# The first layer's last two chunks as Strassen products in an attention-and-MLP kernel

## The chip, the cores and the metric

The kernel runs on one core of a Trainium2 chip. A core has five engines that run side by side, each working through its own list of instructions in order: TensorE (PE; its weight loads are a row of their own, PEld), VectorE (DVE), ScalarE (ACT), GpSimd (POOL) and SyncE (SP, which here only starts transfers). They meet through semaphores. The metric is the device time of one execution in microseconds.

## The reference

The first stage is causal attention with 16 extra "beacon" keys that every query sees; the second is a two-layer perceptron with a leaky ReLU. The attention's output, heads side by side, is the perceptron's input.

```python
B, H, S, Nb, D = (8, 8, 576, 16, 64)
scores = scale * np.matmul(q, k_all.transpose(0, 1, 3, 2))   # k_all: beacons, then keys
scores = np.where(causal, -1000000000.0, scores)
a = np.exp(scores - scores.max(-1, keepdims=True))
a /= a.sum(-1, keepdims=True) + 1e-09
attn = np.matmul(a, v_all)
x = attn.transpose(0, 2, 1, 3).reshape(B * S, H * D)         # 4608 x 512
h = x @ w_in                                                 # 512 x 2048
g = np.maximum(0.01 * h, h)
out = g @ w_out                                              # 2048 x 512
```

## The kernel before

**Attention** goes by pairs of heads: 8 batches of 4 pairs make 32 pairs g, 0 to 31. For each, the transposed keys and queries give scores (L314), ScalarE takes the exponential into a tile of probabilities `aT` (L329, L333; four such tiles, used in turn), GpSimd sets the masked triangles to zero (`affine_select`, L289), and TensorE multiplies the probabilities with the values (L359), in two halves a pair: 12 matmuls, then 18. VectorE divides by the row sums into `x_nat` (L388, L389), which frees the PSUM tile, and SP's queue transposes `x_nat` by DMA into `xT`, the perceptron's input with features on partitions (L417, L422, L425; the last batch has three such transposes a pair).

**The perceptron** goes by nine chunks of 512 tokens, 0 to 8. `up()` makes one 128-row block of the first layer (L442): four matmuls of 512 columns, one for each 128 of the 512 features, into a PSUM tile, which ScalarE takes through the leaky ReLU (Prelu) into `gT` (L450). A chunk has 16 of them. `down()` makes half a product of the second layer. Chunk 0's is plain; for the others Strassen's identity in Winograd's form is used: the left factor (tokens by hidden features) and the right one (hidden features by outputs) are cut into 2 x 2 blocks, and seven products of half size take the place of eight. A product has two `down()`s of eight matmuls with 256 columns (L537). The sums of token blocks that the products need are made from `gT` by VectorE (`token_sums`, L610, four a slice, two slices a chunk); the sums of weight blocks are made once (`weight_sums`). `combine` joins the products: ScalarE copies p1, p4, p5 out of PSUM (L562), VectorE adds (L559), SP stores.

**PSUM** has two `sc` tiles of two banks (2 x 512 floats), for scores, and four tiles of one bank (pool `ps_one`) that all else takes in turn: a value product, an `up()` or a product of the second layer gets the tile that was taken four tiles earlier, once that one is empty.

**The order** is what the program writes (`manual_schedule`): each engine runs its instructions as emitted. From pair 8 on, a list of events with positions in units of pairs is sorted, and between two events `fill()` emits as many `up()`s and `down()`s as an even spread over the batch asks for; `KEPT` = 4 of them are kept over to the next batch. When the list is done, a loop of `fill()` emits what is left: the rest of chunk 6, chunk 7 and chunk 8. `due` is a list of token sums waiting to be emitted, one with each `up()` or `down()`.

Of the kernel before, what the change touches and what calls it, by code (L numbers as in the profile page):

```python
# [8 lines left out]
FP32 = mybir.dt.float32  # L9
BF16 = mybir.dt.bfloat16  # L10
AF = mybir.ActivationFunctionType
# [4 lines left out]
def kernel(  # L16
# [11 lines left out]
    nc = tc.nc  # L28

    B, H, S, D = q.shape  # L30
    NB = beacon_k.shape[2]
    DM = moe_w_in.shape[0]
    DF = moe_w_in.shape[1]
# [4 lines left out]
    NF = DF // 128  # L38
# [411 lines left out]
        nc.scalar.activation(out=gT[i][:, fc, :], in_=acc, func=AF.Prelu, alpha=0.01)  # L450

    HF, HD, HT = NF // 2, DM // 2, 256
    ADD, SUB = ALU.add, ALU.subtract

    def weight_sums(part):
# [13 lines left out]
    def token_sums(i, lo, hi):  # L469
        if i not in sums:  # L470
            sums[i] = [sum_tile(n).rearrange("p (c t) -> p c t", c=HF) for n in range(3)]
        g, s = gT[i], sums[i]
        a11, a12 = g[:, lo:hi, 0:HT], g[:, HF + lo : HF + hi, 0:HT]
        a21, a22 = g[:, lo:hi, HT : 2 * HT], g[:, HF + lo : HF + hi, HT : 2 * HT]
        s1, s2, s4 = (s[n][:, lo:hi] for n in range(3))
        return [
            dict(out=s1, in0=a21, in1=a22, op=ADD),
            dict(out=s2, in0=s1, in1=a11, op=SUB),
            dict(out=a21, in0=a11, in1=a21, op=SUB),
            dict(out=s4, in0=a12, in1=s2, op=SUB),  # L480
        ]

# [21 lines left out]
    def ND(i):  # L504
        return NF if i == 0 else 2 * len(PRODUCTS)
# [44 lines left out]
    def combine(i, n, acc, tiles):  # L550
        lo, hi = tiles[0] * HD, tiles[1] * HD

        def part(name, new=False):
            if new and lo == 0:
                parts[name] = opool.tile([128, 512], FP32, name=name, bufs=1)
            return parts[name][:, lo:hi]

        def add(to, x, y):
            nc.vector.tensor_tensor(out=to, in0=x, in1=y, op=ADD)  # L559

        if n in (1, 4, 5):
            nc.scalar.copy(out=part(f"p{n}", True), in_=acc)  # L562
        if n == 6:
            add(part("u2", True), acc, part("p1"))
        elif n == 2:
            add(part("p1"), acc, part("p1"))
            store(i, 0, 0, tiles, part("p1"))
        elif n == 7:
            add(part("u3", True), acc, part("u2"))
            add(part("p4"), part("u3"), part("p4"))  # L570
            store(i, 1, 0, tiles, part("p4"))
        elif n == 5:
            add(part("u3"), part("u3"), part("p5"))
            store(i, 1, 1, tiles, part("u3"))
            add(part("p5"), part("u2"), part("p5"))
        elif n == 3:
            add(part("p5"), acc, part("p5"))
            store(i, 0, 1, tiles, part("p5"))

    def store(i, half, cols, tiles, c):  # L580
        t0 = i * 512 + half * HT + tiles[0] * 128
        n = tiles[1] - tiles[0]
        nc.sync.dma_start(
            out=out[t0 : t0 + n * 128, cols * HD : (cols + 1) * HD].rearrange("(t p) d -> p t d", p=128),
            in_=c.rearrange("p (t d) -> p t d", t=n),
        )

    done1, done2, at2, ready, turn, first_down, held = [0], [0], [0, 0], [0], [0], [0], [0]

# [17 lines left out]

    def add_due(n=1):
        while due and n:
            nc.vector.tensor_tensor(**due.pop(0)[1])  # L610
            n -= 1

    def add_all(i):
# [16 lines left out]
    def down():  # L630
        add_due()
        if at2[1] == 4:
            add_all(at2[0])
        moe2(*at2)
        done2[0] += 1
        at2[1] += 1
        if at2[1] == ND(at2[0]):
            at2[:] = at2[0] + 1, 0
        turn[0] = 0
# [19 lines left out]
            )  # L659

    NG = B * NPAIR
    KEPT, LEAD = 4, 2

    def has(g):
        return 0 <= g < NG
# [68 lines left out]
    with order:  # L734
        load_first_keys()
        load_beacon_k(0, 2, nc.scalar)
        nc.vector.memset(blank, 0.0)
        nc.vector.memset(ident, 0.0)
        run("l0.0 l1.0")
        make_identity(nc, ident, nomemset=True)  # L740
        make_ones()
        run("l1.1 l2.0 l2.1 V0.0 V0.1 l3.0 l3.1 V0.2 V0.3 V0.4 l4.0 l4.1 i0")
        make_pads()
        unused(13, 256)
        cast_beacon_k(0, 2, nc.scalar.copy)
        beacon_transposes(0, 2)
        unused(13)
        nc.scalar.copy(out=k_nat0[:, :, 0], in_=first_k[0])
        nc.vector.tensor_copy(out=k_nat0[:, :, 1], in_=first_k[1])
        run("q0.1 k0 w2.384 s0.0 m0.0 w3.256 s0.1 q1 s0.2 m0.1 k1 s0.3 m0.2")  # L750
        run("w2.384 s1.0 m1.0 q2 s1.1 k2 w2.384 s1.2 m1.1 w2.384 s1.3 m1.2 W0.0.4 s2.0 m2.0 W0.0.4 s2.1 W0.0.6 q3 l5.0 l5.1 s2.2 k3 w4.384 v0.0 m2.1 s2.3 i1 m2.2 W0.1.4 s3.0 m3.0 v1.0 s3.1 v0.1 s3.2 v1.1 m3.1 l6.0 l6.1 s3.3 x0.1 m3.2")
        run("v2.0 V1.0 V1.1 q4 v2.1 x1 k4.1 v3.0 v3.1 x2.1 s4.0 s4.1 x3 m4.0 V1.2 V1.3 V1.4 l7.0 l7.1 u u s4.2 s4.3 q5 k5 m4.1 m4.2 u o0 u")
        load_beacon_k(2, B, nc.gpsimd)
        run("s5.0 s5.1 m5.0 u u u s5.2 s5.3 q6 k6 m5.1 m5.2 o1 u u s6.0 s6.1 m6.0 u v4.0 u v4.1 y4 N8.0 N8.1 u s6.2 s6.3 q7 k7 m6.1 m6.2 u")
        cast_beacon_k(2, B, nc.gpsimd.tensor_copy)
        run("u v5.0 u v5.1 N9.0 s7.0 s7.1 m7.0 d x5 v6.0 v6.1 T8 d s7.2 s7.3")
        beacon_transposes(2, B)
        run("m7.1 m7.2 N9.1 u b8.2 b9.2 b10.2 b11.2 x6 v7.0 T9 v7.1 d d d N10.0 N10.1 d V2.0 V2.1 x7 t0 T10")


        FIRST = 2 * NPAIR
        COLS = FLAT[NKB]
        TILES = (NG - FIRST) * COLS // 512

        def tile_parts(n):
            at, end, parts = 512 * n, 512 * (n + 1), []
            while at < end:
                r, lo = divmod(at, COLS)
                hi = min(COLS, lo + end - at)
                parts.append((FIRST + r, lo, hi))  # L770
                at += hi - lo
            return parts

        def block(m):
            tiles = [tile_parts(n) for n in range(3 * m, min(3 * m + 3, TILES))]
            for n, parts in enumerate(tiles):
                stretch(parts, apart=n == 0)
            for parts in tiles:
                triangles(parts)

        def has_down():
            return at2[0] < done1[0] // NF

        since = 0
        events = []
        for g in range(FIRST, NG):
            if g > FIRST + 2:
                events.append((g - 3.25, 0, run, ("N%d.0" % g,)))
                events.append((g - 2.95, 0, run, ("N%d.1" % g,)))
            if g > FIRST + 2:  # L790
                events.append((g - 1.75, 0, run, ("T%d" % g,)))
            if g > FIRST + 3:
                events.append((g - 2.5, 0, run, ("b%d.2" % g,)))
            at = g + (2.05 if g % NPAIR == NPAIR - 1 else 2.25)
            events.append((at, 3, value, (g, 0)))
            events.append((at + 0.37, 4, value, (g, 1)))
            events.append((at + 0.38, 5, x_turn, (g,)))
        for m in range((TILES + 2) // 3):
            events.append((FIRST + (0.4 if m else 0.6) + 1536 / COLS * m, 2, block, (m,)))
        ends = [FIRST]  # L800
        for g in range(FIRST, NG):
            events.append((g + 3.5, 2, finish, (g, 2)))
            if g % NPAIR == NPAIR - 1:
                ends.append(g + 3.5)
        for b in range(2, B):
            for n in range(2 if b == 2 else 0, NKB):
                events.append((4 * b - (0.1 if b == 2 else 0.4 - 0.3 * n), 6, load_v_cast, (b, n)))
        events.sort(key=lambda e: e[:2])
        first_down[0] = 4
        w, d0 = 0, done1[0] + done2[0]  # L810
        for at, _, what, args in events:
            while w + 2 < len(ends) and at > ends[w + 1]:
                w, d0 = w + 1, done1[0] + done2[0]
            todo = NF * ready[0] + sum(ND(i) for i in range(ready[0])) - KEPT - d0
            aim = d0 + todo * (at - ends[w]) / (ends[w + 1] - ends[w])
            while done1[0] + done2[0] < aim and fill():
                pass
            if what is block:
                since = done1[0] + done2[0]
            elif what is value:  # L820
                while done1[0] + done2[0] < since + (2 if has_down() else 4) and fill(True):
                    pass
            what(*args)
        while at2[0] < NCH:
            fill()


# [28 lines left out]
```

## Time and profile before

| what | us |
|---|---|
| median of 3 runs | 330.15 (327.78 to 332.76) |
| the profiled execution | 334.24, of which span 332.5 |
| last value product ends | 266.65 |
| chunk 7's first layer, TensorE | 275.38 to 289.20 |
| chunk 8's first layer with chunk 7's second | 290.94 to 315.24 |
| last matmul ends | 329.21 |

The profile is one execution. Its span runs from the first to the last instruction; the execution's own time is 1.74 us more. Busy times are given for each engine, with the idle time ahead of a group of instructions and what ended it. "The chain that ended last" is followed back from the last instruction, each step to what released it. In the timeline a row has the start, the length, the engine, the line of the kernel, the operation, output and inputs, the shapes, and in square brackets how long the engine sat idle before and for whom.

The granted TensorE clock was 0.998 of full speed over the span.

### The profile page before, as it was taken

What the parts mean: (1) busy time and instruction counts of PE and PEld (TensorE: products, weight loads), DVE (VectorE), ACT (ScalarE), POOL (GpSimd) and SP (SyncE); (2) the same over time, 40 slices, a digit from 0 to 9 for tenths busy, and PEclk for the clock granted to TensorE, in tenths of its full rate; (3) what the DMA queues carried; (4) which work ended last, traced back from release to release, by engine and by line L of the source; (5) the groups of instructions that cost most, each with busy time, mean ns of one, the idle gap of its engine ahead of it and who ended that gap; (6) DMA issues with size and microseconds to landing.
All of it is one profiled execution on the core that took longest, in us unless ns stands there. A gap on an engine that the chain in (4) does not pass through costs nothing.

```text
span 332.5 us, 8516 instructions
## 1 busy us (share of the span) xinstructions
PE 325.1 (98%) x3429; PEld 215.8 (65%) x3429; DVE 146.4 (44%) x297; ACT 201.0 (60%) x336; POOL 188.2 (57%) x354
## 2 busy tenths in 40 slices
PE   8999999998999999999999999999999999999995
PEld 5457456444578457855688888656865695566685
DVE  3327245713665254534434535543553552424344
ACT  3757986196883885477756785686467516643510
POOL 8857875989999968656966887667221000000000
PEclk9999999999999999999999999999999999999999
DMA  8999999999999999999999999999621111000203
GB/s 133 143 175 169 124 197 121 134 148 193 165 137 143 178 168 102 162 141 130 124 136 206 139 141 91 197 101 117 98 97 49 38 52 63 2 33 30 67 32 128
DMA packets 155928, 39.93 MB, mean 120 GB/s; under 512 B 143040, under 2 KB 153152, under 8 KB 155888
## 3 DMA queue, kind: packets, MB, share of 16 engines
q0 software_dynamic: 99824, 18.54, 84.1%
q1 hardware_dynamic: 55792, 20.77, 36.9%
q8 instruction: 27, 0.44, 0.6%
q14 instruction: 13, 0.11, 0.2%
q10 hardware_dynamic: 272, 0.07, 0.1%
HBM read 37.22 MB, written 9.44 MB: 140 GB/s over the span
## 4 chain that ended last, share of the span: by engine, by line
PE 81%; DMA 6%; ACT 4%; POOL 4%; DVE 2%; issue 1%; SPq 0%; DVEq 0%; ACTq 0%; POOLq 0%
PE acc L442 32%; PE acc L537 26%; PE av L359 8%; PE sc L314 5%; PE sc L267 3%; ACT aT L333 3%; PE av L645 3%; DMA k_nat<-in_k_dram 3%; PE tp L243 2%; DMA xT<-x_nat 2%; DMA kT<-k_nat 1%; POOL v_aug L214 1%; DVE u L559 1%; POOL k_nat L171 1%; DVE p L559 1%
## 5 line engine op out<-in xcount | busy, mean ns | idle before, releaser
L442 PE MATMUL acc<-xT,w_in_sb 128*128 128x512 bf16 (+1 forms) x640 | 136.6, 358 | 1.0 <-ACT gT L450 0.4
L450 ACT ACTIVATE gT<-acc 128x512 bf16<-128x512 f32 x144 | 83.6, 616 | 53.4 <-PE acc L442 50.9
L289 POOL TENSOR_SCALAR_AFFINE_SELECT aT<-aT 128x256 bf16<-128x256 bf16 (+2 forms) x160 | 64.5, 429 | 63.2 <-ACT aT L329 29.8
L442 PEld LDWEIGHTS <-w_in_sb 128*128 128x128 bf16 x640 | 59.4, 98 | 52.9 <-issue 4.3
L537 PEld LDWEIGHTS <-gT 128*128 128x128 bf16 x512 | 48.7, 98 | 8.4 <-issue 1.2
L333 ACT ACTIVATE aT<-sc 128x1024 bf16<-128x1024 f32 (+3 forms) x64 | 51.8, 895 | 0.0
L537 PE MATMUL acc<-w_out_sb,gT 128*128 128x256 bf16 x384 | 46.2, 273 | 0.0
L359 PEld LDWEIGHTS <-aT 128*128 128x128 bf16 (+1 forms) x960 | 36.9, 98 | 9.0 <-issue 2.6
L537 PEld LDWEIGHTS <-gsum 128*128 128x128 bf16 x384 | 36.7, 98 | 6.8
L329 ACT ACTIVATE aT<-sc 128x512 bf16<-128x512 f32 (+3 forms) x64 | 29.0, 521 | 19.1 <-PE sc L314 19.1
L359 PE MATMUL av<-v_aug,aT 128*128 128x65 bf16 (+1 forms) x960 | 39.6, 195 | 0.9 <-DVE x_nat L389 0.7
L562 ACT COPY p<-acc 128x512 f32<-128x512 f32 (+1 forms) x25 | 14.5, 580 | 39.0 <-PE acc L537 35.3
L388 DVE RECIPROCAL rec<-av 128x6 f32<-128x6 f32 (+1 forms) x64 | 12.0, 187 | 55.9 <-PE av L359 55.6
L171 POOL DMA_DIRECT2D k_nat<-in_k_dram x48 | 34.7, 728 | 1.8 <-DMA v_aug<-in_v_dram 0.7
L171 POOL DMA_DIRECT2D q_nat<-in_q_dram x48 | 34.7, 728 | 0.5 <-issue 0.3
L214 POOL DMA_DIRECT2D v_aug<-in_v_dram x40 | 34.1, 859 | 0.0
L389 DVE TENSOR_TENSOR x_nat<-av,rec 128x384 bf16<-128x384 f32 (+1 forms) x64 | 31.4, 491 | 2.2
L276 ACT ACTIVATE aT<-sc 128x1024 bf16<-128x1024 f32 (+3 forms) x32 | 26.8, 875 | 9.1 <-PE sc L267 8.6
L537 PE MATMUL acc<-w_sum,gsum 128*128 128x256 bf16 x256 | 31.9, 273 | 0.0
L610 DVE TENSOR_TENSOR gsum<-gT 128x1024 bf16<-128x1024 bf16 x16 | 11.3, 703 | 30.1 <-ACT gT L450 30.1
L314 PE MATMUL sc<-qT,kT 64*128 64x80 bf16 (+22 forms) x384 | 22.3, 250 | 1.2 <-DMA kT<-k_nat 1.2
L314 PEld LDWEIGHTS <-kT 64*128 64x128 bf16 x384 | 12.9, 94 | 12.9 <-issue 8.2
(62 smaller groups left out, 235.7 us busy)
## 6 DMA issues: line engine op xcount, KB each, us to landing
out_dram<-p SPq DMA_DIRECT2D x26, 256.0 KB, 3.1
q_nat<-in_q_dram POOLq DMA_DIRECT2D x48, 72.0 KB, 5.4
k_nat<-in_k_dram POOLq DMA_DIRECT2D x48, 72.0 KB, 5.4
v_aug<-in_v_dram POOLq DMA_DIRECT2D x24, 128.0 KB, 6.0
w_in_sb<-in_moe_w_in_dram POOLq DMA_DIRECT2D x2, 1024.0 KB, 10.3
w_out_sb<-in_moe_w_out_dram POOLq DMA_DIRECT2D x2, 1024.0 KB, 12.3
out_dram<-u SPq DMA_DIRECT2D x8, 256.0 KB, 2.7
gsum<-in_q_dram POOLq DMA_DIRECT2D x8, 144.0 KB, 4.8
```

The costliest lines, as they stand in the source:

```text
L171: nc.gpsimd.dma_start(out=t[:, :, par], in_=(q, k)[which][b, 2 * hp + par].rearrange("(t p) d -> p t d", p=NR),)
L214: nc.gpsimd.dma_start(out=dst[lo : ROWS[c], c, :, 0:D], in_=v[b, :, OFF[c] : OFF[c] + n].rearrange("h p d -> p h d"),)
L276: nc.scalar.activation(out=aT[:, :, c0 : c0 + w], in_=sc[:, :, 0:w], func=AF.Exp, scale=0.125)
L289: nc.gpsimd.affine_select(out=view, in_=view, compare_op=ALU.is_ge, fill=0.0, base=128 - n if lo == 0 else 0, channel_multiplier=-1, patte ...
L314: nc.tensor.matmul(out=(sc[par] if apart else sc[:, par])[:, at : at + b - a], lhsT=kT[ps_, c * 128 : (c + 1) * 128], rhs=qT[ps_, q0 : q0 ...
L329: nc.scalar.activation(out=probs[g][:, par, lo:hi], in_=sc[par][:, at : at + hi - lo], func=AF.Exp, scale=0.125)
L333: nc.scalar.activation(out=probs[g][:, :, lo:hi], in_=sc[:, :, at : at + hi - lo], func=AF.Exp, scale=0.125)
L359: nc.tensor.matmul(out=avv[:, n, 0 : D + 1], lhsT=aT[0 : ROWS[c], par, a0 : a0 + 128], rhs=va[0 : ROWS[c], c, 2 * hp + par, :], start=(c = ...
L389: nc.vector.tensor_tensor(out=x_nat[:, t0:t1].rearrange("p t e d -> p (t e) d"), in0=avv[:, :, 0:D], in1=rec[:, n0:n1, None].to_broadcast( ...
L442: nc.tensor.matmul(out=acc[:, lo:hi], lhsT=w_in_cols(fc, j), rhs=xT[:, j, x0 : x0 + hi - lo], start=(j == 0), stop=(j == NJ - 1), skip_gro ...
L450: nc.scalar.activation(out=gT[i][:, fc, :], in_=acc, func=AF.Prelu, alpha=0.01)
L537: nc.tensor.matmul(out=acc[:, lo : lo + HD], lhsT=left(i, n, fc, tile), rhs=right(n, fc), start=(lo == 0 and fc == 0), stop=(fc == HF - 1) ...
```

## The change

Chunks 7 and 8 (`TAIL` = 7 and on) no longer run `up()`. Their first layer is made by the same identity as the second: a chunk's 512 tokens are cut into halves of 256, the 512 features into halves of 256, the 2048 hidden features into halves of 1024. The seven products are made in four slices r, each with two 128-row blocks of either half of the hidden features. `in_first(i, r)` ("A") makes products 1, 6, 5 and 4, `in_second(i, r)` ("B") makes 2, 3 and 7: product 2 is added in PSUM onto 1, 3 onto 5 and 7 onto 6, and product 4 stays in PSUM. A slice's products lie in the two `sc` tiles, which the scores no longer need. The intermediate results p1, p5, u2, u3, c12, c21, c22 lie in float tiles that are cut from the keys' buffer and the fourth probabilities' tile.

The weight sums 5, 6 and 4 are written by GpSimd into the first three probabilities' tiles as these fall free, at positions behind the value products of pairs 28, 29 and 30; sum 7 takes the place of the weights' block b12, after chunk 6's first layer. The token sums of chunk 7's input are made by VectorE, those of chunk 8's by GpSimd.

In `combine`, three of the adds of chunk 7 go to GpSimd; in `token_sums`, one of the four adds of chunks 7 and 8 does. The last pair's `finish` moves from g + 3.5 to g + 2.5, and 12 (`LEFT`) instead of 4 second-layer steps are kept behind attention. What follows is written out as a string: "d" is a `down()`, "A70" is `in_first(7, 0)`.

```diff
-            dict(out=a21, in0=a11, in1=a21, op=SUB),
+            dict(out=a21, in0=a11, in1=a21, op=SUB, eng=nc.gpsimd if i >= TAIL else nc.vector),
...
+        spare = nc.gpsimd if TAIL <= i < NCH - 1 else nc.vector
...
-            add(part("p4"), part("u3"), part("p4"))
+            add(part("p4"), part("u3"), part("p4"), spare)
...
+    def w_in_sums(n):
+        (b11, b21), (b12, b22) = ((w_in_sb[i][:, 0:2], w_in_sb[i][:, 2:4]) for i in range(2))
+        x, y = {5: (b12, b11), 6: (b22, w_t[5]), 4: (b21, w_t[6]), 7: (b22, b12)}[n]
+        nc.gpsimd.tensor_tensor(out=w_t[n], in0=x, in1=y, op=SUB)
...
+        eng.tensor_tensor(out=s1, in0=a21, in1=a22, op=ADD)
+        eng.tensor_tensor(out=s2, in0=s1, in1=a11, op=SUB)
+        eng.tensor_tensor(out=s4, in0=a12, in1=s2, op=SUB)
+        eng.tensor_tensor(out=s3, in0=a11, in1=a21, op=SUB)
...
+    def in_first(i, r):
+        if i not in gT:
+            gT[i] = gpool.tile([128, NF, 512], BF16, name="gT")
+        a, b = (ps_sc.tile([128, 2, 512], FP32, name="sc", tag="sc") for _ in range(2))
+        in_banks[i, r] = a, b
+        in_product(i, 1, 2 * r, a[:, 0], True)
+        nc.scalar.copy(out=temps["p1"], in_=a[:, 0])
+        in_product(i, 6, 2 * r, a[:, 1], True)
+        nc.vector.tensor_tensor(out=temps["u2"], in0=a[:, 1], in1=temps["p1"], op=ADD)
+        in_product(i, 5, 2 * r, b[:, 0], True)
+        nc.scalar.copy(out=temps["p5"], in_=b[:, 0])
+        in_product(i, 4, 2 * r, b[:, 1], True)
...
+        in_product(i, 2, 2 * r, a[:, 0], False)
+        leave(0, 0, a[:, 0])
+        in_product(i, 3, 2 * r, b[:, 0], False)
+        tt(out=temps["c12"], in0=b[:, 0], in1=temps["u2"], op=ADD)
+        leave(0, 1, temps["c12"])
+        in_product(i, 7, 2 * r, a[:, 1], False)
+        tt(out=temps["u3"], in0=a[:, 1], in1=temps["p1"], op=ADD)
+        tt(out=temps["c21"], in0=b[:, 1], in1=temps["u3"], op=ADD)
+        nc.gpsimd.tensor_tensor(out=temps["c22"], in0=temps["u3"], in1=temps["p5"], op=ADD)
+        leave(1, 0, temps["c21"])
+        leave(1, 1, temps["c22"])
+        add_due()
+        if r % 2:
+            due.extend((i, op) for op in token_sums(i, 2 * r - 2, 2 * r + 2))
...
-            events.append((g + 3.5, 2, finish, (g, 2)))
+            at = g + (2.5 if g == NG - 1 else 3.5)
+            events.append((at, 2, finish, (g, 2)))
...
+        for g, n in ((NG - 4, 5), (NG - 3, 6), (NG - 2, 4)):
+            events.append((g + 2.9, 7, w_in_sums, (n,)))
...
-        while at2[0] < NCH:
-            fill()
+        w_in_sums(7)
+        x_in_sums(TAIL, nc.vector)
+        x_in_sums(TAIL + 1, nc.gpsimd)
+        last_chunks("d5 A70 B70 d A71 B71 d A72 B72 d A73 B73 d4")
+        last_chunks("d2 A80 B80 d2 A81 B81 d2 A82 B82 d2 A83 B83 d6 d14")
```

`in_product` is four matmuls of 256 columns (two blocks of 128 hidden features by two of 128 input features); `leave` is the Prelu of a quarter of the slice into `gT` (`leave(0, 0)` first half of the tokens, first half of the hidden features).

## The prediction

> **What bounds the kernel now.** I read the busy shares first, then the chain that ended last, then the timeline of its last 90 us, which is where the change lies.
>
> ```profile
> span 332.5 us, 8516 instructions
> PE 325.1 (98%) x3429; PEld 215.8 (65%) x3429; DVE 146.4 (44%) x297; ACT 201.0 (60%) x336; POOL 188.2 (57%) x354
> ```
>
> TensorE has work all the time. The chain, in order of time, shows that from 255 us on its matmuls alone set the end:
>
> ```profile
> 266.65 8.73 PE acc L537 x80
> 275.38 13.81 PE acc L442 x64
> 289.20 1.75 PE acc L537 x16
> 290.94 0.86 PE acc L442 x4
> 291.81 0.87 PE acc L537 x8
> ...
> 315.24 10.49 PE acc L537 x96
> ```
>
> Columns: start, length, what. L442 is the first layer: chunk 7's 64 matmuls in one piece, 13.81 us (0.216 each), and chunk 8's in groups of four between the second layer's eights (0.87, or 0.109 each). No other engine stands between them, so a saved matmul is worth its full length here, and every wait added to TensorE costs its full length. Three rows of the timeline bear on what is added:
>
> ```profile
> 246.74 0.84 DVE L559 TENSOR_TENSOR u<-u,p 128x512 f32<-128x512 f32 x1 [3.27 <-ACT p L562]
> 247.62 0.69 DVE L559 TENSOR_TENSOR p<-u,p 128x512 f32<-128x512 f32 x1
> 249.01 0.53 PE L359 MATMUL av<-v_aug,aT 128*128 128x65 bf16 x12 [0.36 <-DVE x_nat L389]
> ```
>
> Even now TensorE waits here for a PSUM tile that VectorE empties behind those two adds: no slack. And where VectorE and GpSimd both read SBUF:
>
> ```profile
> 85.47 1.22 DVE L465 TENSOR_TENSOR w_out_sb<-w_out_sb 128x2048 bf16<-128x2048 bf16 x1
> 85.48 3.36 POOL L289 TENSOR_SCALAR_AFFINE_SELECT aT<-aT 128x256 bf16<-128x256 bf16 x4
> 86.60 1.19 DVE L610 TENSOR_TENSOR gT<-gT 128x1024 bf16<-128x1024 bf16 x1
> ```
>
> Four selects take 3.36 us instead of four times 0.41, and the L610 add 1.19 instead of 0.69: they take turns.
>
> **What the Trainium skill says.** "SBUF — State Buffer", section "Who interferes with whom": a VectorE instruction with two SBUF inputs contends with a GpSimd instruction that reads SBUF, and the loser is blocked for the whole instruction. The rows above agree. "GPSIMD Engine Reference", section 3.1: a two-input add of 2048 fp32 elements takes 4497 ns on GpSimd. The trace of before has no such operation. "PSUM — Partial Sum Buffer", section "PSUM bank collisions raise a hardware error", asks for semaphores by bank; the trace can't show it, but it matters below that banks would suffice. "TensorE: Matmul & The Clock Gate", section "What's actually happening": after about 3.4 us idle the array's clock halves. Before has no such gap.
>
> **The change part by part.**
>
> *Fewer matmuls.* Per chunk 64 of 512 columns (13.81 us) become 7 products of 16 with 256 columns: 112 x 0.109 = 12.2. Two chunks: **-3.3 us**.
>
> *The new loop's waits.* A step A then B makes seven products in two `sc` tiles of two banks each. The built order of the changed kernel shows waits by tile, not by bank: product 6's first matmul waits for ScalarE's copy of p1 (other bank), product 4 for the copy of p5, product 2 for VectorE's u2, product 7 for the first Prelu, the next step's product 1 for u3, its product 5 for c21. ScalarE runs in written order, so the next copy of p1 stands behind all four Prelus. Durations: ScalarE's 128x512 copy 0.58 (first end to next start in a queue: 0.50 start to start), Prelu 0.60, VectorE 0.69, four 256-column matmuls issue in 0.44 and end 0.16 after; hand-over 0.03 to 0.04 (ACT starts at 289.23 after the matmul's end at 289.20), 0.10 between dependent VectorE adds (325.75, 326.54). From one start of the p1 copy: copy ends 0.58; product 6 issues 0.62, product 5 issues 1.06, ends 1.66; p5 copied 2.27; product 4 issues 2.31, product 2 2.75, ends 3.35; Prelu ends 3.98; product 7 issues 4.02 to 4.46, ends 4.62; u3 5.34, c21 6.13; third Prelu starts 6.17, fourth 6.67, next p1 copy **7.17**. The fourth Prelu needs GpSimd's c22 (from u3 at 5.34 plus 512/2048 of 4.5 us: 6.5), just in time.
> TensorE's own work in such a period is 28 x 0.109 = 3.05 plus one `d` of 0.87 in chunk 7 (3.92) or two in chunk 8 (4.79). Three periods each: 3 x 3.25 + 3 x 2.38 = 16.9. The step that ends each chunk costs 0.63 + 4.46 - 3.05 = 2.04, twice: 4.1. In chunk 8 a p4 copy of the second layer lies between two steps: 0.5. **+21.5 us.** Nothing hides it: the `d` work is counted as running inside it, and TensorE takes its instructions in order.
>
> *The entry.* Step A70 comes after five `d`, where before ten ran (8.73 us) before chunk 7. The token sums s1 and s2 need the last transpose, which this view of L425 with the SP timeline dates:
>
> ```profile
> 269.89 2.24 SPq L425 DMA_TRANSPOSE xT<-x_nat  x1
> DMA to landing us min/median/max: 2.3/3.0/3.7
> ```
>
> It lands at 269.89 + 3.7 = 273.6; s1 and s2 are two adds of 512 bf16 (0.43 each by the 0.69 and 1.22 of 1024 and 2048), so product 6 starts at 274.55. The last value product ends at 266.65; five `d` (4.36) put product 1 at 271.0 and, without the sums, product 6 at 272.25. That is 2.3 late. VectorE then has s4, s3, two chunk 6 sums and its u2 ahead of step A's u2: 1.5 more. **+3.8 us.** Before, the same landing was covered by 1.8 us.
>
> *Weight sums on GpSimd.* Four adds of 2048 bf16. One-input selects give (0.41-0.32)/(256-160), about 0.94 ns per element, so 2.1 us is the low end, 4.5 (the skill) the high end; an estimate between twice the one-input rate (3.9) and the skill is 4.2, which I take. Each shuts two-input VectorE adds out for that long, and VectorE is in order, so x_nat behind them is late. The first sum is queued while the add at 246.74 runs and takes the turn before the one at 247.62: the PSUM tile awaited at 249.01 comes 4.2 late. The next starts when pair 29's last value product ends, ahead of the token sums of 256.75; TensorE has three more tiles to fill: 1.25. The third follows pair 30's: 3.85 after three first-layer groups (2.6) are used up. The fourth starts as chunk 6's last L442 ends (264.3 before), ahead of the sums at 265.09, and delays the last x_nat, so the transposes and the entry: 3.7. **+13.0 us**; from +5.5 (2.1 each) to +14 (4.5), and 0 if VectorE wins each turn.
>
> *Costed at nothing.* The chunk 7 adds moved to GpSimd (three of about 1.1) lie beside 12 us of chunk 8's second layer; if that cover failed, the stores behind them would be late by 3. The s3 sums on GpSimd (about 2.2) may shut out VectorE's next sum: 0 to 1.9, at two steps. SP's queue keeps its order and every DMA. The regrouped first-layer work beside the last value products keeps its 44 matmuls: within 0.5. The last 14 `d` and the tail are unchanged. Half clock after the three stalls near 4 us: 0 to 5 in all, taken as 0.
>
> Sum: -3.3 + 21.5 + 3.8 + 13.0 = **+35.0**. The profiled execution took 334.24 (span 332.5), 4.1 over the median of the runs, 330.15 (327.78 to 332.76). So span 367.5, and the median 330.15 + 35 = **365**.
>
> **Rivals.**
> 1. *Waits only, no shut-out.* GpSimd's sums are short or lose the turns. For: selects of 0.41 cost VectorE little. Against: 85.48. -3.3 + 21.5 + 3.8 = +22: **352**.
> 2. *Not slower: the engines pass each other by bank.* If product 6 need not await the copy of p1, the copies, Prelus and adds alone repeat: copy p5 to product 3 (1.15), c12 1.87, u3 2.48, c21 3.27, two Prelus, p1 copy ends 4.9. Against 3.92 and 4.79: 3 x 0.98 + 3 x 0.1 = 3.2, which the matmuls pay; only the entry is left: **334**. It decides once a period falls below about 5; the waits in the built order speak against it. With early sums too it would be 327.
> 3. *The change doesn't do what it says*: excluded, the built order has 112 matmuls of 256 per chunk.
>
> **How the numbers follow.** Waits and shut-out 0.60 (likeliest: 365), waits only 0.33, by bank 0.05, by bank with early sums 0.02. The range runs from waits only with a period of 6.6 (352 - 3.4, less 1.5 for a shorter entry: 347) to the sum with half clock and s3 races (365 + 10: 375). About 2%, 6.6 us, is what a measurement here can tell from no change: faster 0.02, same 0.05, slower 0.93.
>
> **What would show it.** Step by step: chunk 7's and 8's p1 copies about 7 us apart; TensorE idle before product 6 for ScalarE, before product 7 for the Prelu; weight-sum rows of about 4 us on GpSimd with VectorE adds stretched beside them and TensorE waiting on x_nat; GpSimd rows of 2 us would take the sum to 357. A period under 5 us makes the whole forecast wrong.

## The result and the profile after

| | before | after |
|---|---|---|
| median of 6 runs, us | 330.08 (327.78 to 332.76) | **371.62** (370.15 to 375.60) |
| ratio to before | | **1.128** (95% interval 1.120 to 1.137) |
| profiled execution, us | 334.24, span 332.5 | 370.53, span 368.8 |
| granted TensorE clock over the span | 0.998 | 0.976 |

The change costs 41.5 us. Some executions of one kernel take over 1.5% longer than its fastest: the ratios leave these out, the medians and ranges here and below are over all, and the profiled execution of before (334.24 against 327.78) is such a longer one. Four lines of the page of after, first; the last two digit rows cut the span into 40 slices of 9.2 us, in tenths (TensorE's busy share, then its granted clock):

```profile
span 368.8 us, 8843 instructions
PE 326.8 (89%) x3525; PEld 225.2 (61%) x3525; DVE 182.5 (49%) x326; ACT 209.3 (57%) x352; POOL 230.3 (62%) x377
...
PE   8999998999999999999999999959684666767786
...
PEclk9999999999999999999999999988988899999999
```

TensorE's busy time over the span hardly changed (326.8 against 325.1 us), so nearly all of the added 36 us of span are idle time, and they begin all at once in slice 27, at 240 us. What it waits for from there on is in the view of its waits, window 240 to 372 us (engine, tile and line that waited, what released it; then total, times, longest, in us):

```profile
PE sc L641 <- ACT kT L658: 10.4, 7, 1.9
PE av L359 <- DVE x_nat L389: 8.9, 3, 4.4
PE sc L641 <- ACT kT L662: 5.8, 8, 0.7
PE sc L641 <- DVE aT L624: 4.6, 1, 4.6
PE sc L641 <- ACT gT L670: 1.7, 7, 0.3
PE acc L538 <- DVE p L560: 1.6, 1, 1.6
PE sc L641 <- DVE kT L660: 1.0, 2, 0.6
```

L641 is a matmul of the new first layer. Four rows are the new loop: TensorE stands before product 6 for the copy of p1 (L658), before product 4 for that of p5 (L662), before product 7 for the first Prelu (L670), before product 2 for u2 (L660). The row of L359 is a value product without a PSUM tile, that of L624 is the entry into chunk 7, that of L560 lies in chunk 8's second layer. Before had 0.7 us of waits for `x_nat` in its whole span and none of the others.

One common point makes the runs comparable more sharply than their medians: the VectorE add of `combine` that waits 3.27 us for a copy of p starts at 246.74 in before and at 240.66 in after. From its start to the end of the span, the **late stretch**, it is 85.76 us before and 128.14 after: +42.4, where the medians have +41.5. (The spans are given to 0.1 us, so a late stretch is no finer than that.) That the add came 6.08 us later in before fits where the two profiled executions stood among their own runs: 4.16 above the one median, 1.09 below the other. In the late stretch TensorE's idle time grows from 3.7 to 37.4 us. Its busy time grows too, from 82.1 to 90.8, though the change takes matmuls away: some of them ran at a lower clock, as shown next.

**The weight sums.** Timeline of after, start, length, engine, what; the first and the third of the four places:

```profile
240.66 4.86 DVE L560 TENSOR_TENSOR u<-u,p 128x512 f32<-128x512 f32 x1 [3.27 <-ACT p L565]
...
240.93 4.05 POOL L607 TENSOR_TENSOR aT<-w_in_sb,w_in_sb 128x2048 bf16<-128x2048 bf16 x1
...
246.95 0.81 PE L359 MATMUL av<-v_aug,aT 128*128 128x65 bf16 x12 [4.38 <-DVE x_nat L389]
...
247.57 3.60 PE L442 MATMUL acc<-xT,w_in_sb 128*128 128x512 bf16 x8
...
262.76 4.34 POOL L607 TENSOR_TENSOR aT<-w_in_sb,aT 128x2048 bf16<-128x2048 bf16 x1 [2.02 <-PE av L359]
263.10 4.54 DVE L728 TENSOR_TENSOR gsum<-gT,gsum 128x1024 bf16<-128x1024 bf16 x1
...
268.34 0.53 PE L359 MATMUL av<-v_aug,aT 128*128 128x65 bf16 x12 [2.98 <-DVE x_nat L389]
...
269.63 3.52 PE L538 MATMUL acc<-w_out_sb,gT 128*128 128x256 bf16 x16
```

While GpSimd makes a sum of 2048 bf16 elements (4.05 to 4.34 us), a VectorE add that took 0.84 before takes 4.86, and one of 0.69 takes 4.54: both end 0.54 us after GpSimd's sum. TensorE's wait follows. The eight first-layer matmuls after the first wait take 3.60 us, and the sixteen of the second layer after the other one 3.52. The same groups in before:

```profile
249.37 1.89 PE L442 MATMUL acc<-xT,w_in_sb 128*128 128x512 bf16 x8
...
264.18 1.91 PE L537 MATMUL acc<-w_out_sb,gT 128*128 128x256 bf16 x16
```

The stretch by stretch view of after, of which the columns that matter here are the window, TensorE's busy time (the first after the length) and the granted clock (after the five busy times), says why:

```profile
240.00:250.00 10.00, 5.62 (x30) 2.49 (x29) 6.82 (x6) 2.92 (x6) 4.97 (x4) 0.78 0.14 38
250.00:260.00 10.00, 10.00 (x82) 5.24 (x81) 3.93 (x4) 6.81 (x12) 4.76 (x5) 0.88 0.15 41
...
280.00:300.00 20.00, 11.70 (x72) 8.21 (x73) 11.52 (x16) 6.33 (x11) 6.36 (x6) 0.83 0.04 14
...
290.00:295.00 5.00, 2.36 (x17) 1.68 (x15) 1.81 (x3) 2.21 (x4) 1.08 (x1) 0.84 0.15 52
295.00:300.00 5.00, 3.76 (x25) 2.68 (x24) 1.98 (x3) 2.31 (x4) 1.27 (x1) 0.82 0.00 0
...
300.00:330.00 30.00, 20.75 (x173) 16.64 (x173) 18.45 (x24) 13.40 (x24) 9.06 (x5) 1.00 0.08 27
```

The clock is 0.78 and 0.88 around the first wait, 0.83 at the entry and in the loop's first steps, and 1.00 from 300 to 330 us, though TensorE is busy only 69% there. Read in windows of half a microsecond, it is 0.50 from about 245.7 to 252.4, 269.5 to 272.6, 283.1 to 286.5 and 293.4 to 296.7 us, and 1.00 between these. TensorE is busy for 13.9 us of the four; half of that, 7.0 us, is my estimate of what the lower clock adds to its busy time.

**The entry and the loop.** The same timeline around product 6 of step A70 (the matmuls at 283.12), and ScalarE's copies of p1 in chunk 7 with one of the waits for them:

```profile
279.02 1.15 POOL L623 TENSOR_TENSOR aT<-xT 128x512 bf16<-128x512 bf16 x1 [5.59 <-DMA xT<-x_nat]
...
280.26 1.42 DVE L623 TENSOR_TENSOR aT<-xT 128x512 bf16<-128x512 bf16 x1 [5.00 <-POOL aT L623]
...
281.78 1.19 DVE L624 TENSOR_TENSOR aT<-aT,xT 128x512 bf16<-128x512 bf16 x1
...
283.12 1.01 PE L641 MATMUL sc<-aT,aT 128*128 128x256 bf16 x4 [4.61 <-DVE aT L624]
...
291.67 0.56 ACT L658 COPY kT<-sc 128x512 f32<-128x512 f32 x1
...
292.29 0.60 PE L641 MATMUL sc<-aT,aT 128*128 128x256 bf16 x4 [1.91 <-ACT kT L658]
...
300.07 0.57 ACT L658 COPY kT<-sc 128x512 f32<-128x512 f32 x1
...
307.51 0.57 ACT L658 COPY kT<-sc 128x512 f32<-128x512 f32 x1
```

VectorE's two sums (L623, L624) take 1.42 and 1.19 where such an add takes 0.42 with GpSimd at rest (run 6, below): GpSimd makes chunk 8's sums beside them. (The row of L623 names GpSimd as the releaser; the chain that ended last has the last transpose, which lands at 280.18.) The copies of p1 stand 8.40 and 7.44 us apart; the last of the four stretches at half clock lies within the longer step.

### The profile page after: what moved, and what is told of

It reads as the page before. It is cut to its first block, busy times and chain, and to the rows that moved or that the text cites. A ratio compares the mean times of both kernels' runs of the same rounds, so it can differ in the third digit from the quotient of the medians.

```text
span 368.8 us, 8843 instructions
## 1 busy us (share of the span) xinstructions
PE 326.8 (89%) x3525; PEld 225.2 (61%) x3525; DVE 182.5 (49%) x326; ACT 209.3 (57%) x352; POOL 230.3 (62%) x377
## 4 chain that ended last, share of the span: by engine, by line
PE 60%; DVE 12%; ACT 9%; issue 6%; DMA 6%; POOL 5%; SPq 1%; POOLq 0%; DVEq 0%; ACTq 0%
PE acc L442 20%; PE acc L538 16%; PE av L359 7%; PE sc L641 5%; PE sc L314 5%; DVE gsum L728 3%; ACT aT L333 3%; DVE u L560 3%; DMA xT<-x_nat 3%; DMA k_nat<-in_k_dram 2%; ACT gT L670 2%; PE sc L267 2%; PE av L763 2%; PE tp L243 1%; DVE kT L684 1%
## 5 line engine op out<-in xcount | busy, mean ns | idle before, releaser
L442 PE MATMUL acc<-xT,w_in_sb 128*128 128x512 bf16 (+1 forms) x512 | 108.7, 357 | 1.3 <-DMA xT<-x_nat 0.5
L289 POOL TENSOR_SCALAR_AFFINE_SELECT aT<-aT 128x256 bf16<-128x256 bf16 (+2 forms) x160 | 61.1, 413 | 57.3 <-ACT aT L329 32.4
L450 ACT ACTIVATE gT<-acc 128x512 bf16<-128x512 f32 x112 | 64.7, 621 | 47.1 <-PE acc L442 46.5
L442 PEld LDWEIGHTS <-w_in_sb 128*128 128x128 bf16 x512 | 47.2, 99 | 41.6 <-issue 6.6
L538 PEld LDWEIGHTS <-gT 128*128 128x128 bf16 x512 | 49.6, 99 | 9.4 <-issue 3.1
L333 ACT ACTIVATE aT<-sc 128x1024 bf16<-128x1024 f32 (+3 forms) x64 | 51.8, 896 | 0.0
L538 PE MATMUL acc<-w_out_sb,gT 128*128 128x256 bf16 x384 | 47.8, 279 | 1.6 <-DVE p L560 1.6
L359 PE MATMUL av<-v_aug,aT 128*128 128x65 bf16 (+1 forms) x960 | 39.5, 195 | 9.5 <-DVE x_nat L389 9.2
L359 PEld LDWEIGHTS <-aT 128*128 128x128 bf16 (+1 forms) x960 | 36.7, 98 | 17.9 <-issue 10.1
L329 ACT ACTIVATE aT<-sc 128x512 bf16<-128x512 f32 (+3 forms) x64 | 29.0, 522 | 19.7 <-PE sc L314 19.1
L686 POOL TENSOR_TENSOR aT<-kT 128x512 f32<-128x512 f32 x8 | 10.2, 1270 | 42.1 <-DVE kT L684 42.1
L565 ACT COPY p<-acc 128x512 f32<-128x512 f32 (+1 forms) x25 | 14.5, 579 | 37.2 <-PE acc L538 32.2
L728 DVE TENSOR_TENSOR gsum<-gT 128x1024 bf16<-128x1024 bf16 x16 | 17.1, 1072 | 21.9 <-ACT gT L450 16.6
L276 ACT ACTIVATE aT<-sc 128x1024 bf16<-128x1024 f32 (+3 forms) x32 | 25.9, 875 | 3.4 <-PE sc L267 3.4
L641 PEld LDWEIGHTS <-aT 128*128 128x128 bf16 x96 | 9.8, 103 | 25.4 <-issue 18.0
```

What stands on the lines that cost most here:

```text
L289: nc.gpsimd.affine_select(out=view, in_=view, compare_op=ALU.is_ge, fill=0.0, base=128 - n if lo == 0 else 0, channel_multiplier=-1, patte ...
L329: nc.scalar.activation(out=probs[g][:, par, lo:hi], in_=sc[par][:, at : at + hi - lo], func=AF.Exp, scale=0.125)
L333: nc.scalar.activation(out=probs[g][:, :, lo:hi], in_=sc[:, :, at : at + hi - lo], func=AF.Exp, scale=0.125)
L359: nc.tensor.matmul(out=avv[:, n, 0 : D + 1], lhsT=aT[0 : ROWS[c], par, a0 : a0 + 128], rhs=va[0 : ROWS[c], c, 2 * hp + par, :], start=(c = ...
L442: nc.tensor.matmul(out=acc[:, lo:hi], lhsT=w_in_cols(fc, j), rhs=xT[:, j, x0 : x0 + hi - lo], start=(j == 0), stop=(j == NJ - 1), skip_gro ...
L538: nc.tensor.matmul(out=acc[:, lo : lo + HD], lhsT=left(i, n, fc, tile), rhs=right(n, fc), start=(lo == 0 and fc == 0), stop=(fc == HF - 1) ...
```

## The experiments

Theory, from the prediction: (1) the four weight sums on GpSimd shut VectorE out, (2) the loop turns at the pace of a chain through three engines, because a wait is by `sc` tile and not by bank, (3) the rest is the entry and smaller stays of VectorE behind GpSimd. Rivals: the whole loss is (2); or a step is that slow because of the adds and copies themselves, whatever the tiles. Late stretches, from the profiles, beside the medians (line numbers in the kernels of the runs can be one or more higher):

| run | edit | late stretch | median (range) | ratio to before (interval) |
|---|---|---|---|---|
| after | | 128.14 | 371.62 (370.15 to 375.60) | 1.128 (1.120 to 1.137) |
| 1 | one-bank tiles | 114.33 | 357.79 (356.98 to 358.56) | 1.086 (1.080 to 1.093) |
| 2 | weight sums on VectorE | 116.11 | 361.69 (356.96 to 365.36) | 1.090 (three fastest runs; no interval) |
| 3 | memsets for the weight sums | 116.12 | 360.37 (358.48 to 363.90) | 1.092 (1.085 to 1.100) |
| 4 | 1 and 2 | 100.52 | 345.51 (343.88 to 348.32) | 1.050 (1.042 to 1.058) |
| 5 | 4, no adds on GpSimd | 96.18 | 338.57 (337.28 to 339.63) | 1.031 (1.027 to 1.035) |
| 6 | 5, later entry | 98.61 | 341.25 (340.42 to 342.93) | 1.040 (1.036 to 1.044) |
| 10 | 6, chunk 6's token sums first | 94.95 | 339.21 (338.30 to 343.07) | 1.032 (1.026 to 1.037) |
| 7 | identity for chunk 8 alone | 86.06 | 329.51 (327.66 to 332.36) | 1.002 (1.000 to 1.005) |
| 8 | 7, token sums behind u2 | 86.44 | 329.71 (328.17 to 335.21) | 1.003 (1.000 to 1.005) |
| 9 | 8, even pieces | 86.75 | 330.67 (328.19 to 335.58) | 1.004 (1.002 to 1.006) |
| 11 | after, chunk 7's adds on VectorE | 126.27 | 372.24 (370.61 to 376.58) | 1.131 (1.125 to 1.137) |

**1. One-bank tiles.** The four banks of a step become four tiles (the pool of the two `sc` tiles is closed when attention is done; `a[:, n]` of a `Two` is its n-th tile):

```diff
-        a, b = (ps_sc.tile([128, 2, 512], FP32, name="sc", tag="sc") for _ in range(2))
+        b00, b01, b10, b11 = (ps_in[0].tile([128, 512], FP32, name=f"in{n}") for n in range(4))
+        a, b = Two(b00, b01), Two(b10, b11)
```

> The changed kernel with the four products of a step in four PSUM tiles of one bank in place of two tiles of two banks; nothing else. Theory (TensorE waits because the waits go by tile): the copies of p1, 7.45 us apart now, come about 5.0 apart in chunk 7 and about 5.3 in chunk 8, TensorE's waits for the p1 and p5 copies (10.4 and 5.8 us) nearly vanish, and the time falls from 371.6 by 3 x 2.4 + 3 x 2.2 + 2 x 1 = 16 to about 356 (351 to 360). Rival (ScalarE and VectorE have so much work in a step that they set the period whatever the waits): the copies stay over 7 us apart and the time stays within 3 us of 371.6.

It took 13.8 us off, 357.8 where 356 was forecast. ScalarE's copies of p1 in chunk 7, in the timeline of this run:

```profile
291.56 0.56 ACT L668 COPY kT<-in 128x512 f32<-128x512 f32 x1
296.63 0.57 ACT L668 COPY kT<-in 128x512 f32<-128x512 f32 x1
302.21 0.57 ACT L668 COPY kT<-in 128x512 f32<-128x512 f32 x1
```

5.07 and 5.58 apart, not 7.44: the arithmetic is the same, so that pace came from the shared tile. In chunk 8, where 5.3 was forecast, they are 7.54, 5.09 and 7.27 apart (8.74, 7.46 and 7.45 in after): there u2 stands in VectorE's queue behind token sums and adds of `combine`, and TensorE waits for it, up to 1.55 us at a time. So the rival has a part of chunk 8: with the tiles apart, the queues' own work is the next limit. The waits for `x_nat` stay at 8.9, the entry's grows from 4.6 to 6.0. The listed waits of TensorE, those for `x_nat` apart, fall from 25.1 to 15.6, by 9.5. The rest is TensorE's busy time in the late stretch, which falls from 90.8 to 86.3: two of the four stretches at half clock, those at 269.5 and 293.4, have no like here.

**2. The weight sums on VectorE**, at the same places (`nc.vector` for `nc.gpsimd` in `w_in_sums`).

> The changed kernel with the four sums of up weights on VectorE in place of GpSimd; same places in the order, nothing else. Theory (a GpSimd sum shuts two-input adds of VectorE out, so x_nat and TensorE's next PSUM tile are late, and the stalls halve the clock): the three waits of TensorE for x_nat (8.9 us) and the lowered clock ahead of the last value product go, some 13 us; four sums of 1.22 on VectorE give 1 to 2 back: about 360 (357 to 363). Rival (the place of the sums in the order is what costs, not their engine): within 3 us of 371.6.

12.0 us off the late stretch. In its timeline a sum costs VectorE 1.22 us, and the value product behind it is on time:

```profile
241.23 1.22 DVE L607 TENSOR_TENSOR aT<-w_in_sb,w_in_sb 128x2048 bf16<-128x2048 bf16 x1
241.46 0.53 PE L359 MATMUL av<-v_aug,aT 128*128 128x65 bf16 x12 [0.36 <-DVE x_nat L389]
```

Waits for `x_nat` drop from 8.9 to 0.4, the entry's from 4.6 to 3.6: 9.5 us, and so much the listed waits fall in all. The other 2.5 are TensorE's busy time, 88.3 in place of 90.8. The clock of 240 to 250 us is 1.00 instead of 0.78, but that of 270 to 280 is 0.64, lower than in after: the gain ahead of the entry is larger than 12.0, and some is lost behind it (run 4).

**3. Memsets for the sums.** Is it GpSimd's reading that shuts VectorE out, or its being busy? Each sum becomes four memsets of the same tile, so products 4, 5, 6 and 7 of the last two chunks are not computed from the weights here.

```diff
-        nc.gpsimd.tensor_tensor(out=w_t[n], in0=x, in1=y, op=SUB)
+        for _ in range(4):
+            nc.gpsimd.memset(w_t[n], 0.0)
```

> The changed kernel with each sum of up weights replaced by four GpSimd memsets of the same tile: the weight sums are left out, so products 4, 5, 6 and 7 of the last two chunks are not computed. GpSimd is about as long busy, but reads no SBUF. Theory of the shut-out by reads: no VectorE add beside a memset is longer than 0.9 us, no wait for x_nat, about 358 (356 to 361). Rival (any long GpSimd instruction delays what stands behind it, or holds VectorE up): as slow as the changed kernel, 369 or more.

The timeline where GpSimd's first 7.39 us of memsets lie:

```profile
240.68 0.84 DVE L560 TENSOR_TENSOR u<-u,p 128x512 f32<-128x512 f32 x1 [3.27 <-ACT p L565]
240.92 7.39 POOL L608 MEMSET aT<- 128x2048 bf16 x4
241.56 0.69 DVE L560 TENSOR_TENSOR p<-u,p 128x512 f32<-128x512 f32 x1
```

GpSimd is busy for longer than with a sum, and VectorE's adds keep their 0.84 and 0.69. So a busy GpSimd does not stretch VectorE's adds; one that reads its operands from SBUF does. What stands behind the memsets in GpSimd's own queue is late, though: chunk 8's input sums and, behind them, c22 of step B70 start only at 272.02 and 276.72, and TensorE's longest wait for a copy of p1 is 3.6 us in place of 1.9. That the late stretch equals run 2's is chance: it is 1.7 us shorter up to product 6 of A70 and as much longer behind it.

**4. Both.**

> Both edits, PSUM tiles of one bank and the weight sums on VectorE. Theory (the two costs lie one behind the other on TensorE's path): the gains add up, 371.6 - 16 - 12 = about 344 (339 to 350), still slower than before. Rival (they overlap, the one hiding the other): 352 or more.

27.6 us off, 1.8 more than the two gains together. Split at the start of product 6 of A70, the late stretch of after is 42.5 + 85.7 us, that of run 1 43.1 + 71.2, of run 2 28.3 + 87.8, of run 4 28.2 + 72.3: the sums cost 14.1 ahead of the entry, the shared tiles 14.5 behind it, and each edit gains nearly in full in its own part when both are made. What run 2 lost behind the entry (2.1) and run 1 ahead of it (0.7) is gone here but for 1.1 behind. 14.8 us to before were left.

**5. No adds on GpSimd.** c22, a token sum of each slice, the three adds of chunk 7 and chunk 8's input sums (these behind step B71) go to VectorE as well.

> PSUM tiles of one bank and weight sums on VectorE as in the run before, and now every other new GpSimd add on VectorE too: c22, the token sums of both layers, the three adds of the second layer; chunk 8's input sums come behind step B71. Theory (what is left over is GpSimd's slower adds on the path and the turns it takes from VectorE): from 345.5, c22 at 0.69 for 1.27 gives 0.6 a step (3), the blocked adds 2 to 3, the entry's two blocked sums 1.6, the wait for GpSimd's add in the last products 1.7: about 336 (333 to 340). Rival (VectorE, with some 4.8 us of adds a step, becomes the bound): 343 or more.

4.3 us more, 338.6 where 336 was forecast. What is left of TensorE's waits: u2 3.3, copy of p1 3.0, entry 2.2.

**6. A later entry**: nine `d` ahead of the first step and none behind the last ("d9 A70 B70 ... A73 B73").

> The same with nine second-layer steps ahead of A70 in place of five, and none left over behind B73. Theory (TensorE's one long wait at the entry is for the last transposes and the two sums, and needs only other work in front): the wait before product 6, 3.5 us at least, goes almost whole; the gap behind B73 costs up to 1: 3 below the run beside it, about 333 (330 to 337). Rival (the wait moves on to the u2 add behind VectorE's queue): within 1 of the run beside it.

It missed by 8 us, and the rival missed as well: slower than run 5 by 2.7. The entry's wait is gone, and another has come, in the last `d` ahead of it:

```profile
269.00 0.42 DVE L624 TENSOR_TENSOR aT<-xT 128x512 bf16<-128x512 bf16 x1 [4.68 <-DMA xT<-x_nat]
...
270.59 0.68 DVE L738 TENSOR_TENSOR gT<-gT 128x1024 bf16<-128x1024 bf16 x1
...
271.33 2.55 PE L539 MATMUL acc<-w_out_sb,gT 128*128 128x256 bf16 x12 [3.15 <-DVE gT L738]
```

The input sums of chunk 7 (L624) are emitted first and wait 4.68 us for the transpose; behind them in VectorE's queue stands the token difference (L738) that product 7 of chunk 6 needs. Its own inputs were there: run 10 makes it earlier.

**10. The same with that difference emitted ahead of the input sums** (`add_all(TAIL - 1)` before `x_in_sums`).

> Both chunks, everything on VectorE, nine pieces of the second layer ahead of the first product, and now chunk 6's last token sums emitted ahead of chunk 7's input sums. Theory: product 7 of chunk 6 no longer waits 3.15 us for the token difference that stood behind the input sums: 338 (336 to 340), no entry wait, no wait of product 7. Rival: the copy of x that VectorE stands on comes no sooner, so another step waits in its place and the time stays at 341.

The late stretch is 3.7 us shorter than in run 6, and no wait in front of product 7 or at the entry. The profiled execution of this run is the longest of its four (343.07), so the span of 341.3 says little here; the median of 339.21 is 2.0 under that of run 6. All of the waits left (u2 4.9 us, p1 3.1, `x_nat` 0.4) but the last are now the loop's.

**7. The identity for chunk 8 alone.** `TAIL = NCH - 1`: chunk 7 goes through `up()`, chunk 8's sums are made beside it, and chunk 7's second layer, 14 `d`, lies between the steps. One-bank tiles, and none of the new adds on GpSimd.

```diff
-    TAIL = NCH - 2
+    TAIL = NCH - 1
...
+        last_chunks("d2 A80 B80 d3 A81 B81 d4 A82 B82 d3 A83 B83 d2 d14")
```

> Strassen's first layer for chunk 8 alone; chunk 7 as in the kernel before. One-bank PSUM tiles, no new work on GpSimd, the weight sums and chunk 8's input sums on VectorE beside chunk 7's first layer, three to four second-layer steps of chunk 7 between two steps and two behind the last. Theory (a saved matmul is worth its time once other work covers the step's chain of about 5 us: 3.05 plus 2.6 to 3.5): 1.6 below the kernel before, ratio 0.995 (0.990 to 1.000). Rival (the chain costs wherever it stands, some 1 us a step): 2 to 4 above the kernel before.

As fast as before, not faster: the ratio is just above the range that was forecast, and below the rival's. With three or four `d` between steps the loop's chain is almost hidden; the only row of waits in the view from 250 us on is:

```profile
PE in L642 <- DVE kT L670: 1.5, 2, 1.2
```

The identity saves one chunk 13.81 - 12.2 = 1.6 us of matmuls. The two waits of that row take 1.5 of it. Measured over the late stretch, TensorE's busy time falls by 1.2 us against before (80.9 from 82.1) and its idle time grows by 1.5.

**8 and 9. Can that wait be had?** In 8 no token sum is emitted ahead of a u2 in the loop; in 9 the pieces are "d2 A80 B80 d4 A81 B81 d4 A82 B82 d2 A83 B83 d2 d14" as well.

> Strassen's first layer for chunk 8 alone, as in the run before it, but the token sums are kept out of VectorE's queue ahead of a u2 (up to three of them stand behind it instead). Theory: what that run lacked is the 1.5 us that TensorE waited for u2; three of the four u2 now have only adds of the second layer ahead of them, so 0.5 to 1.5 us come back: 328 to 329, ratio to before 0.998 (0.995 to 1.001). Rival: the waits were cover for something else (the copy of p1, the Prelus) that ends as late: no change, ratio 1.002.

> The same with the second layer's pieces in even numbers between the steps (2, 4, 4, 2, 2), so that fewer of its adds come in a row ahead of the fourth u2. Theory: TensorE waits for u2 no more, under 0.3 us in all: 327.5 to 328.5, ratio 0.996 (0.993 to 0.999): the identity's own saving of 1.7 us less what is left of the tail. Rival: as above, ratio 1.002.

Neither gained (ratios 1.003 and 1.004): the rival was right. The last step of run 8:

```profile
307.61 0.60 PE L642 MATMUL in<-xT,w_in_sb 128*128 128x256 bf16 x4 [0.52 <-ACT kT L668]
...
309.30 0.68 DVE L670 TENSOR_TENSOR kT<-in,kT 128x512 f32<-128x512 f32 x1
310.04 0.60 PE L642 MATMUL in<-aT,w_in_sb 128*128 128x256 bf16 x4 [1.35 <-DVE kT L670]
```

The u2 (L670) still stands behind four adds of `combine`, so product 7 waits for it, and TensorE, no longer held up before, now reaches product 2 ahead of the copy of p1 (L668): 1.8 us of waits in all. In 9 it is the other way round, 1.5 for the copy and 0.5 for u2. In these two orders a moved add showed up as another's wait. None of these versions beats the kernel before.

**11. The adds of chunk 7's `combine` back on VectorE**, the rest as in after (`spare = nc.vector`).

> The changed kernel with one edit undone: the three adds of chunk 7's combination that the change moved to GpSimd are on VectorE again. Theory: TensorE's last wait of 1.6 us for an accumulator of the second layer goes: 370.0 (369 to 371), ratio to before 1.1236 where the change has 1.1283. Rival, as the prediction had it: the adds lie beside TensorE's work on either engine, no change (371.6).

The place, in after and then in this run:

```profile
356.31 1.26 POOL L560 TENSOR_TENSOR p<-u,p 128x512 f32<-128x512 f32 x1
...
357.61 0.69 DVE L560 TENSOR_TENSOR p<-acc,p 128x512 f32<-128x512 f32 x1 [5.80 <-POOL p L560]
...
358.35 3.65 PE L538 MATMUL acc<-w_out_sb,gT 128*128 128x256 bf16 x32 [1.56 <-DVE p L560]
```

```profile
358.63 3.66 PE L538 MATMUL acc<-w_out_sb,gT 128*128 128x256 bf16 x32
```

In after, VectorE's add waits for GpSimd's third, and TensorE for the PSUM tile which that add empties; in run 11 it doesn't wait, and the late stretch is 1.87 us shorter. The median was forecast to fall by 1.6 and did not (372.24 against 371.62), but with ranges of six us it cannot show so little: the trace alone does.

## Why the prediction was right, and where its terms were off

It said 365 (347 to 375) and slower; 371.62 is inside. The sum of 35.0 is 7 us short of the late stretch's 42.4; the range had room for that. Point by point:

- **TensorE has no slack, every wait counts in full**: right. The waits taken away in runs 2, 4, 5 and 10 came back as time.
- **Fewer matmuls, -3.3**: twice 1.6 is 3.2, and the matmuls went (128 of 512 columns against 224 of 256 more), but TensorE's busy time in the late stretch grew by 8.7 (the clock, below, and the ends of many short groups of matmuls).
- **Weight sums on GpSimd, +13.0**: the mechanism is right (runs 2 and 3: 12.0 us in all, 14.1 ahead of the entry in run 2), and so is a sum's length, 4.2 against 4.05 to 4.34. One detail is not: the add that was already running was held, not the next one. It had started 0.27 us ahead of the sum. By place: 4.2, 1.25 and 3.85 were forecast for the first three stalls; the waits are 4.4 (0.4 of it there before), 1.5 and 3.0. The fourth, forecast at 3.7 ahead of the entry, was much smaller: from the last value product's start to product 6's it took 10.14 us, 3.8 more than the prediction's 6.32 without sums, where the fourth sum and the entry together were to add 6.0.
- **Half clock after the stalls, "0 to 5 in all, taken as 0"**: a term mis-sized. From the common add to the last value product (265.93 before, 272.98 after) the time grew by 13.1 us, where three stalls forecast 9.3 and their waits measure 8.9. What is left of the 13.1, over 4 us, is in the matmuls of the two stretches at half clock: 3.60 for 1.89, 3.52 for 1.91 and two smaller groups, 4.2 in all. There is more of it after the entry: the period of 8.40, where the next is 7.44. Over the whole late stretch, entry and loop included, the estimate is 7.0 us of TensorE's busy time, where the term had 0 to 5.
- **The loop, +21.5**: right in its mechanism, which run 1 shows, and in the places of the waits within a step; the two that it named for the next step's products 1 and 5 cost nothing, as its chain had it. The period was 7.17 by the sum and 7.44 to 7.46 measured where nothing else disturbed it. Of that difference, 0.11 has built up by the third Prelu (6.28 after the copy, not 6.17), and the rest comes behind it, where c22 ends late: "512/2048 of 4.5 us", 1.1, is 1.27 on the page (L686). With the period of 8.40 and an add of u in chunk 8 that took 2.61 us beside a token sum on GpSimd, chunk 7's loop took 2.1 us more than forecast, chunk 8's 1.8 more.
- **The entry, +3.8**: up to product 6 the entry (2.3) and the fourth sum (3.7) were to add 6.0, and the two added 3.8; that this is the entry's own number is chance. Two errors met here: the transpose landed 2.37 us after its start (277.81 to 280.18), not 3.7, and VectorE's two sums took 1.42 and 1.19, not 0.43 each, since GpSimd's sums for chunk 8 shut VectorE out here as well. The prediction counted that shutting-out for the weight sums and left it out for these.
- **Chunk 7's adds on GpSimd, "costed at nothing"**: wrong, 1.6 us. The prediction named chunk 8's second layer as cover and looked to the stores behind the adds; what is behind them first is VectorE's next add into the same tile, and with it TensorE's accumulator. Run 11 shows it.
- **The rival of waits only (352)**: not so; the sums cost at least 12 us of themselves. **The rival by bank**: its waits were not those of this kernel, but its period of 4.9 was a fair forecast for run 1's chunk 7 (5.07 and 5.58), and too short for its chunk 8 (5.09 to 7.54).

The late stretch's +42.4 is then 13.1 to the last value product, 3.8 to product 6, and 25.5 from there: 19.7 as forecast (the loop's 21.5, the matmuls' -3.3 and the 1.5 of the entry that lie behind product 6), 2.1 and 1.8 more in the two loops, 1.6 in the tail, and 0.3 that I can't place.

The "SBUF — State Buffer" page of the Trainium skill, section "Who interferes with whom", carried a term of 13 us that the trace of before could only hint at, and the runs agree with it: VectorE was blocked for the whole of the other's instruction by a GpSimd that reads (the sums of after), not by one that only writes (run 3). "GPSIMD Engine Reference", section 3.1, gives 4497 ns for an fp32 add; the bf16 adds here take 4.05 to 4.34 us and the measurement decides.

## What to carry to other kernels

An identity that saves 12% of the matmuls of a stage is bought with copies, adds and Prelus between them; write down the chain from one step's first copy to the next and compare it with TensorE's work in a step, and fill the gap with independent matmuls before counting the saving (4 us of work against a chain of 7.4 lost here, and with enough between the steps the saving was cancelled by a 1.5 us wait). Give each PSUM bank a tile of its own where two engines alternate on them. Work moved to an "idle" GpSimd is not free if it reads its operands from SBUF: list the VectorE adds that lie beside it, and what is queued behind them. These are lessons of this kernel's runs; where other queues are fuller or emptier, the limits can lie elsewhere.

## What the runs showed that I had not expected

- The granted clock was 0.50 or 1.00, and no length of a single wait decides which. In after it fell to 0.50 with the waits of 4.38, 2.98 and 4.61 us, but also at 293.4, behind 6.9 us at 1.00 in which no wait was longer than 1.91. Run 1 has the same third wait (2.99 at 268.88) and stayed at 1.00 behind it. In run 5 a wait of 2.23 was enough; in run 10 the clock was 0.50 from 290 to 294 with no wait over 1.30 in the 40 us before, while after stayed at 1.00 from 300 to 330, with waits of 1.9 and TensorE busy 69%. The prediction's "about 3.4 us idle" does not sort these cases; what does stays open here. Matmuls took about twice as long in such a stretch, so a wait can cost more than its length.
- Two `TENSOR_TENSOR`s that meet do not share: VectorE's 4.86 us for an add of 0.84 is GpSimd's 4.05 and its own. GpSimd loses time as well: its difference of 1024 elements took 2.12 us at 352.89 in after, with VectorE idle, and 2.57 to 2.63 at its three other places there and at 351.96 in run 11, with VectorE adds beside it.
- The two main causes gained 13.8 and 12.0 us when removed alone and 27.6 together. Such a sum hides where the gains lie: by stretch they are 14.5 behind the entry and 14.1 ahead of it, and each run alone gave a little back in the other's part.
